# Scratch stores from ScalarE's DMA ring, scratch laid out anew, and weight pairs of four v and five o in a recurrent attention kernel

## The chip, the cores and the metric

The kernel runs on one core of a Trainium2 chip. The metric is the device time of one execution in microseconds (us), lower is better. Each timed execution is one run; profiles come from one profiled execution each. Engines go by their names in the profile: PE is TensorE's matmuls and PEld its weight loads, ACT is ScalarE, DVE VectorE, POOL GpSimd, SP SyncE. A load has *landed* when the last of the 16 increments of its semaphore has come; the trace shows 16 for each load and doesn't name the DMA engines that they come from.

## The reference

Two parts share an input `x` of 2048 rows by 1024. Part A is a recurrence over 64 segments of 32 rows: each segment puts eight memory rows, the first eight output rows of the segment before, in front of its own 32. Part B is a gated feed-forward layer. A gate mixes both.

```python
mem = mem0                                        # 1 x 8 x 1024
for s in range(64):                               # 2048 rows / 32
    h = concat([mem, x[:, 32*s:32*s+32]])         # 40 rows
    q, k, v = h @ Wq, h @ Wk, h @ Wv              # 32 heads of 128: three 1024 x 4096 weights, bf16
    p = softmax(mask(q @ k.T * scale))
    o = (p @ v) @ Wo                              # 4096 x 1024
    mem = o[:, :8]
    outs.append(o[:, 8:])
b = (gelu(x @ w_gate) * (x @ w_up)) @ w_down      # 1024 -> 3584 -> 1024
out = g * a + (1 - g) * b
```

The four weights of part A are 8 MB each and every segment needs all of them; only the memory rows wait for the segment before.

## The kernel before

Each of the four weights is cut into 16 pieces of 0.5 MB: half `r` (16 heads) times row block `i` (0 to 7). The kernel keeps them in 52 slots of SBUF: 40 serve one piece each, and 12 serve a pair of pieces, half 0 and half 1 of the same block. `PAIRS` names which blocks of each weight are paired. The halves change places every other segment, so that a paired slot is loaded once a segment: 12 loads, 6 MB.

```python
PAIRS = {"k": (0, 2), "q": (0,), "v": (0, 1, 2, 3, 4), "o": (0, 1, 2, 3)}

def seq(m, r):            # order of the blocks: paired ones first in the first half, last in the second
    ...
    return p + f if r == 0 else f + p
walk = both(0) + one("v", 0) + both(1) + [x for y in zip(one("o", 0), one("v", 1)) for x in y] + one("o", 1)

def at_step(p, s):
    m, r, i = walk[p]
    return (m, r ^ (s % 2), i)
...
def fetch(n):             # the load of a slot's next piece, on SyncE
    ...
    op("sp", lambda e: e.dma_start(dst(t, k), src(k)), wr=[t.r()], lane=lane)

def spent(k):             # called after the matmuls of a piece
    n = home[k]
    done[n] += 1
    if done[n] < len(uses[n]) and uses[n][done[n]] != k:
        fetch(n)
```

A segment has 64 steps of matmuls (`walk`). The k and q pieces are steps 0 to 15 and 24 to 39, the first v half 16 to 23, the second v half alternates with the first o half in steps 40 to 55, and the second o half is 56 to 63. A slot is loaded again right after the step that used its first piece. So a v pair has some 30 steps until its second piece is needed, while an o pair is freed at step 40 or later and needed from step 59 or 60. The o pairs have the shortest lead of all.

Four intermediate results go through scratch in HBM, all stored by GpSimd:

```python
qk_scr = nc.dram_tensor("qk_scr", [128, NSEG, 4, 128], BF16)
o_scr = nc.dram_tensor("o_scr", [NSEG, 128, 2, 128], BF16)
...
def store_v(u, G, st):
    op("pool", lambda e: e.dma_start(v_scr[4 * G:4 * G + 4, :, u].rearrange("s i (g j) c -> g (s i) (j c)", g=4), st[:, :]), ...)
def o_store(s=s):         # behind step 60
    op("pool", lambda e: e.dma_start(o_scr[s].rearrange("p u c -> p (u c)"), oRc[:, :, :, :].rearrange("p u c x -> p (u c x)")), ...)
for p in range(64):
    run(at.get(p, []))
    proj(p, s)
... # a_bf <- PB[XO] by ACT and DVE; transposed by PE into the next segment's input
def a_store(s=s):
    op("pool", lambda e: e.dma_start(a_scr[s].rearrange("r (g c) -> g r c", g=4), a_bf[:, :]), ...)
```

## Time and profile before

| kernel before | value |
|---|---|
| runs | 2225.03 to 2231.35 us, median 2227.73 of 3 |
| span of the profiled run, granted clock | 2225.5 us, 0.990 |
| recurrence, 64 segments | about 110 to 1640 us |
| period of a segment | 24.48 us |

The prediction below shows the windows of the stages and the chain. Here are more views of the kernel before. The first is from its page: the granted clock of TensorE (PE) in 40 slices, in tenths; the groups of the v and o projections (L800 and L811), with busy time, mean ns of one, idle time just before them and what ended most of it; and the DMA queues (q1 is fed by SyncE, q0 by GpSimd, q10 by ScalarE), with packets, MB and their share of the 16 engines.

```profile
PEclk9999999999999999999999999999999999999999
...
q1 hardware_dynamic: 216240, 483.68, 62.2%
q0 software_dynamic: 22400, 40.56, 5.6%
q10 hardware_dynamic: 144, 0.26, 0.1%
...
L800 PE MATMUL pb<-sl,hT 128*32 128x512 bf16 x8192 | 728.1, 382 | 49.1 <-DMA sl<-in_A_Wv_dram 37.0
L811 PE MATMUL pb<-sl,oT 128*32 128x256 bf16 x8192 | 352.8, 276 | 85.0 <-DMA sl<-in_A_Wo_dram 47.6
```

Most DMA traffic is the weight loads on q1 (820 of 0.5 MB, 430 of 529 MB). PE waits for v and for o loads, and for both not long (37.0 and 47.6 us in all). The waits of PE and of its weight loads (PEld) show the same; the numbers are total us, times, and the longest. A weight load and a matmul can wait for the same transfer, so the two engines' rows are not to be added.

```profile
PEld pb L800 <- DMA sl<-in_A_Wv_dram: 61.4, 85, 2.0
PEld pb L811 <- DMA sl<-in_A_Wo_dram: 56.7, 54, 2.5
PE pb L754 <- DVE vA L679: 17.4, 29, 1.8
```

### The profile page before, as it was taken

The page shows a single profiled execution, that of the slowest core. Times are in us where ns is not written, and L with a number is a line of the kernel's source. Part 1 is how long each engine was busy: PE and PEld are TensorE (multiplying, and loading weights), DVE is VectorE, ACT ScalarE, POOL GpSimd, SP SyncE. Part 2 cuts the span into 40 slices and gives each one's busy share as a digit, 9 for nine tenths or more (in the row PEclk, how much of TensorE's full clock was granted, in tenths as well). Part 3 has the DMA queues.
Part 4 walks back from the last instruction along what each step waited for, and adds up shares of the span by engine and source line. Part 5 has one row for each costly group of instructions (what it writes and reads, how often), then busy time and mean ns, then how long its engine had stood idle before and what let it go on. Part 6 is the DMA issues. An engine that isn't in the chain of part 4 may idle for free.

```text
span 2225.5 us, 77508 instructions
## 1 busy us (share of the span) xinstructions
PE 2008.3 (90%) x38220; PEld 936.1 (42%) x32556; DVE 1016.7 (46%) x2248; ACT 597.7 (27%) x1266; POOL 431.1 (19%) x776
## 2 busy tenths in 40 slices
PE   7878888988898888888988898899888999999999
PEld 4334444444444434444444444444444424343343
DVE  6434444444444444444444454444444516354362
ACT  4322222222222222222222232222222303122130
POOL 7221222221222222122222222222221000000000
PEclk9999999999999999999999999999999999999999
DMA  9988887888788878888888888788889400001000
GB/s 365 356 287 278 298 292 274 287 302 290 263 292 305 286 265 289 288 294 271 301 289 280 272 310 296 267 294 305 279 287 369 164 34 29 30 25 34 20 29 20
DMA packets 239111, 529.46 MB, mean 238 GB/s; under 512 B 46760, under 2 KB 79784, under 8 KB 238784
## 3 DMA queue, kind: packets, MB, share of 16 engines
q1 hardware_dynamic: 216240, 483.68, 62.2%
q0 software_dynamic: 22400, 40.56, 5.6%
q8 instruction: 278, 4.55, 0.8%
q10 hardware_dynamic: 144, 0.26, 0.1%
q14 instruction: 49, 0.40, 0.1%
HBM read 490.68 MB, written 33.55 MB: 236 GB/s over the span
## 4 chain that ended last, share of the span: by engine, by line
PE 57%; DMA 29%; DVE 9%; issue 2%; ACT 2%; SPq 1%; POOL 0%; POOLq 0%; DVEq 0%; ACTq 0%
DMA sl<-in_A_Wo_dram 18%; PE pb L462 16%; PE pb L800 11%; PE pb L783 9%; DMA sl<-in_A_Wk_dram 6%; PE pb L811 5%; PE pb L1153 4%; PE pb L690 4%; PE pb L830 3%; DMA sl<-in_A_Wv_dram 2%; PE pb L849 1%; DVE pb L726 1%; PE pb L1131 1%; DVE st L725 1%; DVE st L731 1%
## 5 line engine op out<-in xcount | busy, mean ns | idle before, releaser
L800 PE MATMUL pb<-sl,hT 128*32 128x512 bf16 x8192 | 728.1, 382 | 49.1 <-DMA sl<-in_A_Wv_dram 37.0
L811 PE MATMUL pb<-sl,oT 128*32 128x256 bf16 x8192 | 352.8, 276 | 85.0 <-DMA sl<-in_A_Wo_dram 47.6
L783 PE MATMUL pb<-sl,hT 128*32 128x512 bf16 x4096 | 401.2, 382 | 0.0
L800 PEld LDWEIGHTS pb<-sl,hT 128*32 128x32 bf16 x8192 | 215.5, 97 | 405.2 <-issue 249.9
L811 PEld LDWEIGHTS pb<-sl,oT 128*32 128x32 bf16 x8192 | 208.6, 97 | 174.2 <-issue 58.2
L830 PE MATMUL pb<-sl,hR 128*32 128x512 bf16 x3072 | 221.4, 387 | 11.8 <-ACT stv L676 6.0
L777 POOL COPY oRc<-oT 128x128 bf16<-128x128 bf16 x128 | 97.7, 763 | 648.3 <-DVE oT L679 648.3
L676 ACT ACTIVATE tok<-pb 128x512 bf16<-128x512 f32 x192 | 114.7, 598 | 269.5 <-PE pb L800 255.8
L462 PE MATMUL pb<-xT,wg 128*128 128x512 bf16 x768 | 183.2, 382 | 4.2 <-DMA wg<-in_B_w_gate_dram 4.2
L462 PE MATMUL pb<-xT,wu 128*128 128x512 bf16 x768 | 182.4, 381 | 0.0
L679 DVE CAST stg<-pb 128x512 bf16<-128x512 f32 x128 | 86.3, 674 | 165.1 <-PE pb L783 165.1
L1153 PE MATMUL pb<-wd,GT 128*32 128x512 bf16 x1568 | 152.2, 379 | 0.0
L783 PE MATMUL pb<-wd,GT 128*32 128x512 bf16 x1568 | 152.2, 379 | 0.0
L450 ACT ACTIVATE s<-pb 128x512 f32<-128x512 f32 x112 | 66.9, 597 | 291.2 <-PE pb L462 291.2
L451 DVE SCALAR_TENSOR_TENSOR tp<-s,pb 128x512 f32<-128x512 f32 x112 | 76.8, 685 | 122.8 <-ACT s L450 122.4
L679 DVE CAST a_bf<-pb 128x128 bf16<-128x128 f32 x64 | 18.7, 292 | 245.2 <-ACT a_bf L676 245.2
L676 ACT ACTIVATE oT<-pb 128x256 bf16<-128x256 f32 x256 | 84.3, 381 | 124.7 <-PE pb L766 124.7
L462 PEld LDWEIGHTS pb<-xT,wg 128*128 128x128 bf16 x768 | 75.1, 98 | 96.9 <-issue 8.2
L679 DVE COPY qT<-pb 128x512 bf16<-128x512 bf16 x128 | 54.4, 425 | 133.3 <-ACT kT L676 133.3
L729 ACT ACTIVATE E<-pb 128x320 bf16<-128x320 f32 x128 | 56.0, 437 | 220.4 <-DVE pb L726 220.4
L830 PEld LDWEIGHTS pb<-sl,hR 128*32 128x32 bf16 x3072 | 79.7, 97 | 83.0 <-issue 19.6
L462 PEld LDWEIGHTS pb<-xT,wu 128*128 128x128 bf16 x768 | 75.5, 98 | 91.6 <-issue 1.8
(110 smaller groups left out, 2265.4 us busy)
## 6 DMA issues: line engine op xcount, KB each, us to landing
sl<-in_A_Wv_dram SPq DMA_DIRECT2D x331, 512.0 KB, 8.8
sl<-in_A_Wo_dram SPq DMA_DIRECT2D x268, 512.0 KB, 7.0
sl<-in_A_Wk_dram SPq DMA_DIRECT2D x142, 512.0 KB, 6.7
sl<-in_A_Wq_dram SPq DMA_DIRECT2D x79, 512.0 KB, 7.1
qkr<-qk_scr SPq DMA_DIRECT2D x63, 128.0 KB, 8.1
qk_scr<-fqk POOLq DMA_DIRECT2D x30, 256.0 KB, 6.8
wd<-in_B_w_down_dram SPq DMA_DIRECT2D x7, 1024.0 KB, 14.9
xq_scr<-xTp SPq DMA_DIRECT2D x4, 1024.0 KB, 16.8
```

Of the source, the lines that this page charges most:

```text
L450: op("act", lambda e: e.activation(s1[:, :], hg, ACTF.Square, scale=SQ), rd=[BK(bg)], wr=[s1.r()])
L451: op("dve", lambda e: e.scalar_tensor_tensor(out=t[:, :], in0=s1[:, :], scalar=1.0, in1=hg, op0=ALU.add, op1=ALU.mult), rd=[BK(bg), s1.r() ...
L462: ins = e.matmul(PB[bk][:, 0:FB], lhsT=w[:, kc, cc:cc + 128], rhs=x[:, :, :, kc, :].rearrange("p t i c -> p (t i) c"), start=(kc == 0), st ...
L676: op("act", lambda e: e.activation(o, i, ACTF.Copy), rd=rd, wr=wr)
L679: op("dve", lambda e: e.tensor_copy(o, i), rd=rd, wr=wr)
L690: ins = e.transpose(to, t[:, j * 128:(j + 1) * 128], ident[:, :])
L777: op("pool", lambda e: e.tensor_copy(oRc[:, u, :, :].rearrange("p c (g j) -> p g j c", g=4), diag), rd=[oT.r()], wr=[oRc.r(128 * u, 128 * ...
L783: return e.add_instruction(mybir.InstMatmult(name=nc.get_next_instruction_name(), start_tensor_calc=start, stop_tensor_calc=stop, tile_siz ...
L800: ins = again(e, g, *at, one, end) if k[0] == "q" else e.matmul(*at, start=one, stop=end)
L811: ins = e.matmul(PB[XO][32 * g:32 * g + 32, 0:256], lhsT=oT[:, gp_, 2 * jj + hh, 0:32], rhs=w[:, c:c + 256], start=(r == 0 and one and hh ...
L830: ins = e.matmul(PB[b][32 * g:32 * g + 32, :], lhsT=h[:, k[2], :], rhs=w[:, g * 512:(g + 1) * 512], start=(n == 0), stop=(n == 7))
L1153: ins = again(e, q, *a, j == 0, j == NJ - 1) if hf else e.matmul(*a, start=(j == 0), stop=(j == NJ - 1))
```

## The change

The intent: take the stores off GpSimd's software ring and issue them from ScalarE (ACT); lay out the q/k scratch so that each partition is stored as one row of 2 KB, and the o scratch so that each is read as one row of 1 KB (a q/k read becomes two rows of 512 B where it was one of 1 KB); and move one pair from v, for which PE waits 61 us, to o. The number of loads stays 12.

```diff
-        qk_scr = nc.dram_tensor("qk_scr", [128, NSEG, 4, 128], BF16)
+        qk_scr = nc.dram_tensor("qk_scr", [NG, 2, 128, 4, 256], BF16)
-        o_scr = nc.dram_tensor("o_scr", [NSEG, 128, 2, 128], BF16)
+        o_scr = nc.dram_tensor("o_scr", [NG, 2, 128, 4, 128], BF16)
 ... (the q/k and o reads follow the new layouts)
-        PAIRS = {"k": (0, 2), "q": (0,), "v": (0, 1, 2, 3, 4), "o": (0, 1, 2, 3)}
+        PAIRS = {"k": (0, 2), "q": (0,), "v": (0, 1, 2, 3), "o": (0, 1, 2, 3, 4)}
 ...
-        def store_v(u, G, st):
-            op("pool", lambda e: e.dma_start(v_scr[...]...
+        def store_v(u, G, st, eng="act"):
+            op(eng, lambda e: e.dma_start(v_scr[...]...
-        def store_qk(u, G, st):
-            op("pool", lambda e: e.dma_start(qk_scr[:, 4 * G:4 * G + 4, 2 * u:2 * u + 2, :]...
+        def store_qk(u, G, st, eng="act"):
+            op(eng, lambda e: e.dma_start(qk_scr[G, u].rearrange("p i c -> p (i c)"), ...
 ... (the stores of the prologue stay on "pool")
             def o_store(s=s):
-                op("pool", lambda e: e.dma_start(o_scr[s].rearrange("p u c -> p (u c)"), ...
+                op("act", lambda e: e.dma_start(o_scr[s // 4, :, :, s % 4, :].rearrange("u p c -> p u c"), ...
             def a_store(s=s):
-                op("pool", lambda e: e.dma_start(a_scr[s].rearrange("r (g c) -> g r c", g=4), a_bf[:, :]), ...
+                op("act", lambda e: e.dma_start(a_scr[s].rearrange("r (g c) -> g r c", g=4), a_bf[:, :]), ...
```

More of the change, by code (lines that the diff above doesn't have):

```diff
@@ L532, in load_qk @@
         def load_qk(s):
-            op("sp", lambda e: e.dma_start(qkr[:, :, :, :].rearrange("p u m c -> p (u m c)"), qk_scr[:, s].rearrange("p m c -> p (m c)")),
+            op("sp", lambda e: e.dma_start(qkr[:, :, :, :].rearrange("p u m c -> p u (m c)"),
+                                           qk_scr[s // 4, :, :, s % 4, :].rearrange("u p c -> p u c")),
                rd=[("D", "qk", s // 4, u) for u in range(2)], wr=[qkr.r()], lane="qkr")
@@ L663, in load_oR @@
         def load_oR(Q, u, t=oR):
-            op("pool", lambda e: e.dma_start(t[:, :, :].rearrange("p (s i) x -> p s (i x)", i=NB),
-                                             o_scr[4 * Q:4 * Q + 4, :, u, :].rearrange("s p c -> p s c")),
+            op("pool", lambda e: e.dma_start(t[:, :, :].rearrange("p a x -> p (a x)"), o_scr[Q, u].rearrange("p s c -> p (s c)")),
                rd=[("D", "o", s) for s in range(4 * Q, 4 * Q + 4)], wr=[t.r()], lane="oR")
@@ L867, in fill_put @@
                     [BK(TT)], [r])
-        def store_v(u, G, st):
-            op("pool", lambda e: e.dma_start(v_scr[4 * G:4 * G + 4, :, u].rearrange("s i (g j) c -> g (s i) (j c)", g=4), st[:, :]), rd=[st.r()],
-               wr=[("D", "v", G, u)], lane="fv")
-        def store_qk(u, G, st):
-            op("pool", lambda e: e.dma_start(qk_scr[:, 4 * G:4 * G + 4, 2 * u:2 * u + 2, :].rearrange("p i m y -> p i (m y)"),
-                                             st[:, :, :, :].rearrange("p i m y -> p i (m y)")),
-               rd=[st.r()], wr=[("D", "qk", G, u)], lane="fq")
+        def store_v(u, G, st, eng="act"):
+            op(eng, lambda e: e.dma_start(v_scr[4 * G:4 * G + 4, :, u].rearrange("s i (g j) c -> g (s i) (j c)", g=4), st[:, :]), rd=[st.r()],
+               wr=[("D", "v", G, u)], lane=f"fv{eng}")
+        def store_qk(u, G, st, eng="act"):
+            op(eng, lambda e: e.dma_start(qk_scr[G, u].rearrange("p i c -> p (i c)"), st[:, :, :, :].rearrange("p i m y -> p (i m y)")),
+               rd=[st.r()], wr=[("D", "qk", G, u)], lane=f"fq{eng}")
         def mm0(m, u, b, t, G=0, h=hR):
@@ L882, in mm0 @@
             if m == "v":
-                store_v(u, G, t)
+                store_v(u, G, t, "pool")
         def tr0(m, u, t, b, G=0):
@@ L892, in tr0 @@
             if m == "q":
-                store_qk(u, G, b)
+                store_qk(u, G, b, "pool")
         def rest_k(u):
@@ L1008, in o_store @@
             def o_store(s=s):
-                op("pool", lambda e: e.dma_start(o_scr[s].rearrange("p u c -> p (u c)"), oRc[:, :, :, :].rearrange("p u c x -> p (u c x)")),
+                op("act", lambda e: e.dma_start(o_scr[s // 4, :, :, s % 4, :].rearrange("u p c -> p u c"),
+                                                oRc[:, :, :, :].rearrange("p u c x -> p u (c x)")),
                    rd=[oRc.r()], wr=[("D", "o", s)], lane="sto")
@@ L1037, in a_store @@
             def a_store(s=s):
-                op("pool", lambda e: e.dma_start(a_scr[s].rearrange("r (g c) -> g r c", g=4), a_bf[:, :]), rd=[a_bf.r()],
+                op("act", lambda e: e.dma_start(a_scr[s].rearrange("r (g c) -> g r c", g=4), a_bf[:, :]), rd=[a_bf.r()],
                    wr=[("D", "a", s)], lane="st")
```

## The prediction

> **What bounds the kernel now.** I began with the table of windows, which cuts the span into its stages. Its columns are the window in us, its length, busy time of PE, weight loads, DVE, ACT and POOL with instruction counts, the granted clock, the busy share of the DMA engines, and GB/s.
>
> ```profile
> 0.00:110.00 110.00, 88.39 (x700) 42.49 (x668) 59.08 (x92) 40.74 (x74) 51.58 (x60) 0.97 0.97 361
> 110.00:1640.00 1530.00, 1352.79 (x31751) 666.68 (x27776) 695.78 (x1749) 427.51 (x974) 348.98 (x661) 0.99 0.84 287
> 1640.00:1720.00 80.00, 66.01 (x1084) 33.09 (x987) 35.14 (x74) 20.24 (x41) 11.86 (x21) 0.94 0.98 340
> 1720.00:2225.50 505.50, 501.08 (x4698) 193.86 (x3127) 226.67 (x333) 109.19 (x178) 18.65 (x34) 1.00 0.13 46
> ```
>
> The second row is the 64-segment recurrence, and all of the change lies there. PE is busy 1352.8/1530 = 88%, so 12%, or 177 us (2.8 us a segment), is the most that any change of transfers can give. In the feed-forward tail PE is at 99%; nothing of the change acts there.
>
> Next, one segment in the same view:
>
> ```profile
> 1051.20:1054.00 2.80, 2.67 (x72) 1.47 (x64) 0.46 (x2) 0.86 (x3) 1.24 (x3) 1.00 0.21 69
> 1057.00:1060.00 3.00, 3.00 (x80) 1.42 (x64) 0.97 (x3) 1.19 (x2) 0.29 (x1) 1.00 0.93 272
> 1063.00:1066.00 3.00, 3.00 (x83) 1.79 (x76) 2.00 (x5) 1.70 (x4) 0.97 (x2) 1.00 1.02 403
> 1045.00:1048.00 3.00, 2.29 (x64) 1.27 (x68) 2.38 (x9) 0.78 (x3) 0.00 (x0) 1.00 1.04 392
> ```
>
> The DMA engines are full (0.93 to 1.04) in all but one stretch, 1051.2 to 1054.0, at the turn from one segment to the next. The chain of waits that ended last has the same shape: one load of output weights (Wo) nearly every segment.
>
> ```profile
> by line: DMA sl<-in_A_Wo_dram 18.5%; PE pb L462 16.1%; PE pb L800 11.5%; PE pb L783 8.6%; DMA sl<-in_A_Wk_dram 5.6%; PE pb L811 5.1%; PE pb L1153 3.8%; PE pb L690 3.6%; PE pb L830 2.7%; DMA sl<-in_A_Wv_dram 2.4%; issue 2.4%; PE pb L849 1.2%
> ...
> 1043.26 7.84 DMA sl<-in_A_Wo_dram
> ```
>
> Those 7.8 us are mostly time spent queued behind other loads. I averaged issues and landings of the 12 weight loads (0.5 MB each) over the 64 segments. Counted from the first k load, the k,q,k loads are issued at 0, 0.39, 1.07 us and land at 4.80, 7.39, 8.90; the five v loads are issued at 3.8 to 6.1 and land at 10.83, 12.24, 13.64, 15.03, 16.41; the four o loads are issued at 12.4 to 14.2 and land at 17.95, 19.43, 20.83, 22.36. Then 2.27 us pass to the next first k load; the period is 24.6 us. So when the first o load is issued, the fifth v load still has 4.0 us to go: the queue never runs dry, and **the bound is the total of bytes through a busy queue plus one bubble per segment**. In the bubble PE finishes the output projection, ACT and DVE copy it out, it is transposed into the next input, the first k step frees its slot, and the first packets come some 1 us later.
>
> [...] of the v store issued at 751.08, twelve of 16 increments came after 1.86 to 2.27 us and four after 4.17 to 4.44. [...] the median SyncE packet took 18 ns at 256 B, 27 at 512 B, 46 at 1 KB, 84 at 2 KB and 159 at 4 KB.
>
> **The change, part by part.**
> *Stores leave GpSimd.* By the order of instructions, 187 issues move from POOL to ACT (64 o, 64 a, 30 v, 29 k/q: 2.9 a segment). A POOL issue took 0.57 to 0.78 us; POOL is 19% busy and not in the chain, so freeing 187 x 0.65 = 122 us of it is worth about 0. On ACT an issue should cost about what SyncE needs, 0.35 to 0.6 us; ACT is busy 28% of this stage. The o store comes ahead of the copy of a, where ACT has waited:
>
> ```profile
> ACT a_bf L676 <- PE pb L811: 217.0, 64, 4.8
> POOL qk_scr L874 <- DVE fqk L679: 89.0, 29, 4.6
> ```
>
> that is 217/64 = 3.4 us each segment; one or two issues (up to 1.2 us) fit. The a store comes after the copy into the next input, with about 2.9 us until ACT's next copy. Cost: 0.
>
> *The same bytes, on other engines.* From GpSimd, o and v stores moved in the bubble, free. From ACT they start about 0.5 us earlier and meet the tail of the o loads. v: 128 KB on four engines is 32 packets of 1 KB each, 32 x 46 ns = 1.5 us, in about half the segments; perhaps 0.2 us of it lies ahead of the last o landing: 0.1 us on average. o: 256 packets of 256 B over 16 engines, 16 x 18 ns = 0.3 us, of which 0.05. a: 32 packets of 512 B on each of four engines, 32 x 27 = 0.86 us, where it was four packets of 4 KB, 4 x 159 = 0.64, [...] 0.1 to 0.2 us. Together about +0.3 us a segment at most, x64 = 19 us; I take half, **+10 us**, as the end of the busy stretch is set by the slowest of 16 engines, which need not be these.
>
> *The layouts.* k/q store: 512 rows of 512 B become 128 of 2 KB; o reads: 512 of 256 B become 128 of 1 KB. But GpSimd's packets were already merged to 4 KB (9,840 of them on its queue), so this saves little. On the way back, the q/k read goes from 128 x 1 KB to 256 x 512 B, 16 x 27 - 8 x 46 = +64 ns a segment, after the o loads, in the bubble: 0. k/q bytes, 256 KB in half of the segments, still meet the k and v loads: 0.
>
> *Pairs.* One v load fewer and one o load more per segment: 12 loads still. The o rows are 2 KB: 2 x 84 = 168 ns per 4 KB against 159. In the landings above, v loads stand 1.39 us apart and o loads 1.49. So +0.1 us x 64 = **+6 us**. Back the other way, the last v load lands 1.4 us earlier; PE waited for v 37 us and its weight loads 61, but in most segments the o wait that follows simply gets longer by as much. In the chain, only about four segments hang on v: 4 x 0.7 = **-3 us**. The fifth o slot is freed two steps (some 0.5 us) after the fourth, and its load is queued behind four others, so the later issue costs 0. Would the queue run dry? The fourth v load lands at 15.0 and the first o load is issued at 12.4 [...]: a margin of 0.6 us, enough on average.
>
> Sum: 10 + 6 - 3 = **+13 us**, 2241. That adds only costs that I can see, and relieving GpSimd's software ring may give back what I can't; I take 10 us off for that. This is a judgement, not a reading. **2231 us.**
>
> **Rivals.** *A, [...]* If the a and v stores all fall on the same four engines, their lag (0.86 + 0.75 on average) counts in full: +1.0 us x 64 = +64 us, 2290. For it: every load waits for its slowest engine. Against it: half of this falls in the bubble. *B, the software ring was slowing the loads.* 2.5 to 5 us after the first k load, just after the a store, the loads run at about 200 GB/s, and at 380 to 400 later. If leaving GpSimd ended that, it would give about 1.1 us x 64 = -70 us, 2160. Against it: while the k/q store moves, 6 to 8 us after the first k load, its packets take 159 ns and loads beside it run at full pace, so stores from GpSimd alone do not make the dip; and it is there in all four phases. *C, ACT becomes late.* If an issue takes over 1.5 us, the copy of a is late by the rest: +0.5 us, +32 us. Against it: the 3.4 us of idle time. *D, o is the wrong matrix to pair.* Its lead, from slot freed to use, is the shortest. If the queue runs dry before o, one more load of 1.4 us is exposed in part of the segments, say a third: +30 us, 2258.
>
> **Range and chances.** 2% is 44.6 us, or 0.7 us in each segment. My parts are a third of that; only A or B in full reaches it. I give 2231 us, 2200 to 2262, with 0.06 faster, 0.87 same and 0.07 slower.
>
> **What would show it.** Right: the period stays at 24.3 to 25 us; the Wo wait still leads the chain, and v waits shrink while PE's o waits grow; the turn of segments keeps its hole of about 3 us; POOL's issues are gone and ACT's busy time is unchanged. a and v stores from ACT post twelve increments at once. Wrong: the first k load lands over 0.7 us later (A) or the 200 GB/s dip is gone (B); ACT's copy of a starts late after an issue (C); the DMA share drops between the v and the o loads (D).

## More of the kernel before

The timeline of SyncE's queue in one segment, whose first k load was issued at 1029.20 us, has this row for its o loads (start, duration of the four issues):

```profile
1041.65 1.98 SPq L378 DMA_DIRECT2D sl<-in_A_Wo_dram  x4
```

So the o loads are asked for 12.45 us after the first k load: at that time their slots come free.

## The result and the profile after

The changed kernel takes **2335.75 us** (median of four runs, 2331.7 to 2346.05), where the kernel before takes 2226.38 in the same rounds (2218.8 to 2231.35). The ratio is 1.050, with a 95% interval of 1.045 to 1.055: slower by 5%. A ratio is the mean time of one kernel's runs over that of the other's of the same rounds, so it is not quite the ratio of the medians quoted. Executions over 1.5% slower than the fastest of the same kernel are left out of the means. The profiled run has a span of 2344.3 us, where before had 2225.5: +118.8.

The windows of the stages, kernel after, with the columns explained in the prediction:

```profile
110.00:1740.00 1630.00, 1390.26 (x31480) 668.55 (x27544) 687.19 (x1736) 427.50 (x965) 214.26 (x475) 0.95 0.80 267
1830.00:2344.00 514.00, 507.79 (x4838) 198.62 (x3270) 229.20 (x338) 110.87 (x181) 18.67 (x34) 1.00 0.15 53
```

Cut there, the window of the recurrence is 1630 us long instead of 1530. The cuts are by eye, but the loads confirm them: from the first k load of the last segment to the end it is 565.7 us before and 566.1 after, so all of the +118.8 lies in the recurrence. Three columns of the first row moved: the granted clock from 0.99 to 0.95, the DMA share from 0.84 to 0.80, and PE's busy time from 1353 to 1390 us for slightly fewer instructions. The page of the kernel after, with the lines that answer to those of before:

```profile
PEclk9989999999999999999999999999988999999999
...
q1 hardware_dynamic: 232640, 484.20, 60.5%
q10 hardware_dynamic: 34136, 20.19, 3.0%
q0 software_dynamic: 8592, 20.49, 2.4%
...
DMA sl<-in_A_Wo_dram 22%; PE pb L462 15%; PE pb L800 14%; PE pb L783 10%; PE pb L811 5%; PE pb L690 4%; PE pb L1153 4%; PE pb L830 2%; DMA sl<-in_A_Wk_dram 2%; DVE pb L726 1%; DVE st L725 1%; PE pb L849 1%; DVE st L731 1%; DMA qkr<-qk_scr 1%; DVE tB L742 1%
...
L800 PE MATMUL pb<-sl,hT 128*32 128x512 bf16 x8192 | 751.5, 394 | 4.8 <-DMA sl<-in_A_Wk_dram 2.6
L811 PE MATMUL pb<-sl,oT 128*32 128x256 bf16 x8192 | 365.4, 277 | 153.8 <-DMA sl<-in_A_Wo_dram 142.0
```

The stores did move: 20 MB went from q0 to q10. The same 8192 matmuls of L800 take 394 ns on average where they took 382, though one digit a slice hides most of the lower clock. The idle time before v matmuls went from 49 to 5 us, that before o matmuls from 85 to 154, and the o load has 22% of the chain instead of 18%. The waits of the kernel after:

```profile
PEld pb L811 <- DMA sl<-in_A_Wo_dram: 161.1, 127, 2.8
PE pb L811 <- DMA sl<-in_A_Wo_dram: 142.0, 150, 2.6
PE pb L754 <- DVE vA L679: 62.6, 63, 2.0
PEld pb L800 <- DMA sl<-in_A_Wv_dram: 1.4, 5, 0.4
ACT a_bf L676 <- PE pb L811: 286.4, 60, 7.0
```

The wait for v is gone, as the change meant. The wait of L754 (attention) for DVE's copy of v grew at the same time, from 17.4 us to 62.6; that the one became the other isn't shown. The wait for o tripled. ACT still waits for PE before its copy of `a`, 286.4 us in all, so its new issues don't hold it up.

One segment of the kernel after, whose first k load was issued at 1045.03 us, in the timeline of SyncE's queue and then in windows:

```profile
1056.81 2.99 SPq L378 DMA_DIRECT2D sl<-in_A_Wo_dram  x5
```

```profile
1054.00:1056.80 2.80, 2.60 (x60) 1.36 (x56) 2.35 (x7) 1.58 (x4) 0.32 (x1) 1.00 0.99 399
1056.80:1059.00 2.20, 2.20 (x84) 1.70 (x80) 1.18 (x3) 0.27 (x1) 0.68 (x2) 1.00 0.61 181
1059.00:1062.00 3.00, 2.40 (x60) 1.25 (x48) 2.36 (x8) 0.82 (x2) 0.00 (x0) 1.00 1.02 387
1065.00:1068.00 3.00, 1.34 (x34) 0.55 (x32) 0.00 (x0) 0.11 (x1) 0.15 (x1) 1.00 0.60 163
```

From 1056.8, when the first o load is issued, to 1059.0 the engines are busy for only 0.61 of the time and move 181 GB/s, with 399 just ahead and 387 just after. The lost bytes come back at the end: at 1065 to 1068 PE is busy for 1.34 of 3.00 us, waiting for the last o loads. In the kernel before, where the first o load was issued at 1041.65, the same view has

```profile
1042.00:1045.00 3.00, 2.95 (x100) 1.99 (x88) 1.78 (x4) 0.44 (x1) 0.28 (x2) 1.00 0.94 342
```

and 1.04 for 1045 to 1048 (shown in the prediction).

To see it over all segments, I averaged over segments 4 and later the times at which loads land, in us after the first k load is issued. This table is worked out from the traces (e1, e9 and e13 are experiments below). Its last column counts the stretches in which PE was granted half its clock: in before each of the 5 lasts 3.41 us; in after 34 last 3.41, three 6.83 and one 10.24.

| kernel | first o issued | last v landed | o loads landed | period | half-clock windows |
|---|---|---|---|---|---|
| before (5 v, 4 o) | 12.25 | 16.32 | 17.79, 19.26, 20.66, 22.19 | 24.48 | 5 |
| after (4 v, 5 o) | 12.68 | 14.92 | 17.10, 18.98, 20.74, 22.29, 23.82 | 26.33 | 38 |
| e1, pairs alone | 12.77 | 15.14 | 17.23, 19.12, 20.91, 22.40, 23.86 | 26.4 | 38 |
| e9, e1 with PE kept busy | 12.18 | 14.77 | 16.70, 18.43, 20.05, 21.62, 23.09 | 25.55 | 2 |
| e13 (3 v, 6 o) | 12.83 | 13.96 | 16.96, 18.63, 20.66, 22.21, 23.63, 25.18 | 27.95 | 56 |

The fourth v load lands at 14.93 us before and 14.92 after: up to there nothing is lost. The remaining five loads then take 7.26 us before (22.19 - 14.93) and 8.90 after. That is 1.64 us a segment, or 105 us in 64; the other 0.2 us of the period is the turn from the last o landing to the next k issue (2.29 us before, 2.50 after). The rate of the loads in the same time base:

```
GB/s of the weight loads, by the start of a 0.5 us bin after the first k issue (worked out from the traces)
          11.0  11.5  12.0  12.5  13.0  13.5  14.0  14.5  15.0
before     389   372   399   406   368   321   297   333   349
after      398   367   290   193   132   121   168   251   326
e1         400   382   329   248   173   149   181   249   308
e9         392   356   313   218   165   195   259   328   349
e13        267   185   119    78    60    77   135   230   311
```

Before has a dent of a quarter at 13.5 to 14.5; after has a hole of two thirds. In the segment shown above, the 16 increments of the fourth v load and of the first o load came at these times:

```
us after its own issue (worked out from the trace of the kernel after)
v, issued 1050.07   6.98 7.11 7.15 7.31 7.32 7.33 7.36 7.46 7.63 7.70 7.92 7.95 8.29 8.49 9.03 9.28
o, issued 1056.81   3.29 3.31 3.32 3.33 3.34 3.37 3.48 3.49 3.51 3.54 3.59 3.74 3.77 3.88 4.02 4.90
```

The first increment of v came at 1057.05, half of them by 1057.5, the last at 1059.35. The o load had been issued before any of this, and still its first increment did not come before 1060.10. On average over the segments the first increment of v comes at 12.56 us and half of them have come at 13.18; the first o packet starts at 13.76, 1.06 us after its issue.

### The profile page after: what moved, and what is told of

It reads as the page before. It is cut to its first block, busy times and chain, and to the rows that moved or that the text cites. A ratio compares the mean times of both kernels' runs of the same rounds, so it can differ in the third digit from the quotient of the medians.

```text
span 2344.3 us, 77525 instructions
## 1 busy us (share of the span) xinstructions
PE 2057.8 (88%) x38218; PEld 944.3 (40%) x32556; DVE 1014.3 (43%) x2248; ACT 601.1 (26%) x1266; POOL 294.1 (13%) x589
## 4 chain that ended last, share of the span: by engine, by line
PE 58%; DMA 28%; DVE 10%; ACT 2%; issue 1%; POOL 0%; SPq 0%; ACTq 0%; POOLq 0%; DVEq 0%
DMA sl<-in_A_Wo_dram 22%; PE pb L462 15%; PE pb L800 14%; PE pb L783 10%; PE pb L811 5%; PE pb L690 4%; PE pb L1153 4%; PE pb L830 2%; DMA sl<-in_A_Wk_dram 2%; DVE pb L726 1%; DVE st L725 1%; PE pb L849 1%; DVE st L731 1%; DMA qkr<-qk_scr 1%; DVE tB L742 1%
## 5 line engine op out<-in xcount | busy, mean ns | idle before, releaser
L800 PE MATMUL pb<-sl,hT 128*32 128x512 bf16 x8192 | 751.5, 394 | 4.8 <-DMA sl<-in_A_Wk_dram 2.6
L811 PE MATMUL pb<-sl,oT 128*32 128x256 bf16 x8192 | 365.4, 277 | 153.8 <-DMA sl<-in_A_Wo_dram 142.0
L783 PE MATMUL pb<-sl,hT 128*32 128x512 bf16 x4096 | 422.6, 403 | 0.0
L800 PEld LDWEIGHTS pb<-sl,hT 128*32 128x32 bf16 x8192 | 219.7, 100 | 372.4 <-issue 296.1
L811 PEld LDWEIGHTS pb<-sl,oT 128*32 128x32 bf16 x8192 | 199.2, 97 | 260.6 <-DMA sl<-in_A_Wo_dram 161.1
L830 PE MATMUL pb<-sl,hR 128*32 128x512 bf16 x3072 | 228.0, 400 | 11.1 <-ACT stv L676 7.0
L895 POOL COPY kT<-qkr 128x128 bf16<-128x128 bf16 x128 | 37.7, 295 | 676.1 <-PE pb L719 484.1
```

What stands on the lines that cost most here:

```text
L783: return e.add_instruction(mybir.InstMatmult(name=nc.get_next_instruction_name(), start_tensor_calc=start, stop_tensor_calc=stop, tile_siz ...
L800: ins = again(e, g, *at, one, end) if k[0] == "q" else e.matmul(*at, start=one, stop=end)
L811: ins = e.matmul(PB[XO][32 * g:32 * g + 32, 0:256], lhsT=oT[:, gp_, 2 * jj + hh, 0:32], rhs=w[:, c:c + 256], start=(r == 0 and one and hh ...
L830: ins = e.matmul(PB[b][32 * g:32 * g + 32, :], lhsT=h[:, k[2], :], rhs=w[:, g * 512:(g + 1) * 512], start=(n == 0), stop=(n == 7))
```

## The experiments

Fifteen kernels were run, all correct. The first question is which part of the change costs the time; then why.

### Which part: e1, e2, e14, e15

**e1: the pairs alone**, on the kernel before.

```diff
-        PAIRS = {"k": (0, 2), "q": (0,), "v": (0, 1, 2, 3, 4), "o": (0, 1, 2, 3)}
+        PAIRS = {"k": (0, 2), "q": (0,), "v": (0, 1, 2, 3), "o": (0, 1, 2, 3, 4)}
```

> The kernel before with nothing but the weight pairs changed to 4 v and 5 o; all stores stay on GpSimd, scratch layouts as before. Theory 1 (the load queue runs dry between the fourth v load and the first o load, and starts up slowly again; the longer wait at the end of the segment then also costs the PE clock): it carries nearly all of the loss, 2310 to 2340 us, with the DMA rate falling under 200 GB/s some 12.5 to 14 us after the first k load, and a granted clock of 0.95 to 0.97. Theory 2 ([...] ScalarE late because it issues): this kernel is about 2232 us, as the prediction's sum has +6 for the pairs.

Measured: 2330.62 us, ratio 1.049 (1.045 to 1.053), half-clock windows and landings like those of after (table above).

**e2: stores and layouts**, the whole change with `PAIRS` put back.

```diff
-        PAIRS = {"k": (0, 2), "q": (0,), "v": (0, 1, 2, 3), "o": (0, 1, 2, 3, 4)}
+        PAIRS = {"k": (0, 2), "q": (0,), "v": (0, 1, 2, 3, 4), "o": (0, 1, 2, 3)}
```

> The changed kernel with the weight pairs put back to 5 v and 4 o: stores on ScalarE's ring and the new scratch layouts. Theory 1: within 1% of the kernel before, 2215 to 2245 us, clock 0.98 to 0.99. Theory 2: 2300 us or more, with the o loads landing later and the first k load late.

Measured: 2229.86 us, ratio 1.003 (1.001 to 1.006). The window of its recurrence has the length, the DMA share and the clock of before:

```profile
110.00:1640.00 1530.00, 1354.18 (x31716) 670.75 (x27756) 695.72 (x1747) 430.85 (x972) 215.23 (x478) 0.99 0.84 287
```

So the pairs carry +109 us (0.0488 x 2225) and the rest +7. The one line of the change that alters neither the number of loads, nor their bytes, nor any engine's work is the one that counts.

**e14 and e15** split the rest, with five rounds each: the new layouts with all stores left on GpSimd, and the old layouts with the stores on ACT.

```diff
 # e14 on the kernel before: qk_scr, o_scr and their reads as in the change, and
+        def store_v(u, G, st, eng="pool"):
+        def store_qk(u, G, st, eng="pool"):
 # e15 on the kernel before: PAIRS, qk_scr, o_scr and reads untouched, and
+        def store_v(u, G, st, eng="act"):
+        def store_qk(u, G, st, eng="act"):
-                op("pool", ...o_scr...)   -                op("pool", ...a_scr...)
+                op("act", ...o_scr...)    +                op("act", ...a_scr...)
```

> The new scratch layouts alone, stores on GpSimd and pairs 5 v and 4 o as before. By the prediction's sum 0; fewer rows for the software ring might give a little: 2215 to 2232 us (0.995 to 1.003 of the kernel before).

> The stores on ScalarE's ring alone, old layouts and pairs. The two parts together took 1.003 (e2). [...] this one is 1.003 to 1.006 and the layouts alone at or below 1.000; if the layouts make it, this one is 1.000.

Measured: 2228.59 us, 0.998 (0.996 to 1.001), and 2225.43 us, 0.998 (0.995 to 1.000). Neither can be told from the kernel before, and the two don't add up to the +7 us of e2. So of the stores and layouts together no more can be said than that they are worth less than 0.6% either way. No version beats the kernel before.

### Is it the number of o pairs: e3, e4, e13

One rival to a queue that runs dry is that an o load is simply dearer than a v load (its rows in HBM are shorter: in before the median packet of q1 took 84 ns at 2 KB, so 168 for 4 KB, and 159 at 4 KB). Then each o pair more should cost, and each one fewer should gain.

```diff
-        PAIRS = {"k": (0, 2), "q": (0,), "v": (0, 1, 2, 3, 4), "o": (0, 1, 2, 3)}
+        PAIRS = {"k": (0, 2), "q": (0,), "v": (0, 1, 2, 3, 4, 5), "o": (0, 1, 2)}      # e3
+        PAIRS = {"k": (0, 2, 4), "q": (0,), "v": (0, 1, 2, 3), "o": (0, 1, 2, 3)}      # e4
+        PAIRS = {"k": (0, 2), "q": (0,), "v": (0, 1, 2), "o": (0, 1, 2, 3, 4, 5)}      # e13
```

> The kernel before with the pairs moved the other way, 6 v and 3 o. Theory 1: nine loads stand ahead of the first o load, so the queue can't run dry; the sum of bytes is the same, so 2205 to 2235 us; the rate between v and o stays over 300 GB/s. If instead an o pair is dear by itself (2 KB rows, the shortest time from slot freed to use), each one fewer gives back what one more cost: some 100 us faster, about 2120 us.

Measured: 2231.81 us, 1.002 (0.999 to 1.005). No gain, so an o load as such is not dear. The rate stays above 370 GB/s from the v loads to the o loads, so here the queue doesn't run dry at all. The waits of PE's weight loads show why there is none: the wait only changed the matrix, from 57 us for o and 61 for v before to

```profile
PEld pb L800 <- DMA sl<-in_A_Wv_dram: 169.2, 189, 2.3
...
PEld pb L811 <- DMA sl<-in_A_Wo_dram: 3.6, 6, 1.2
```

> The kernel before with one v pair given to k: 3 k, 4 v, 4 o. v has four pairs as in the changed kernel, but eight loads stand ahead of the first o load as in the kernel before. Theory 1 (what counts is how much is queued ahead of the o loads): 2210 to 2245 us. If the loss comes from having only four v pairs (order of v work on TensorE): 2310 to 2340 us.

Measured: 2257.61 us, 1.015 (1.013 to 1.017). This missed its range from 2210 to 2245 by some 12 us. With four v and four o pairs the o loads are issued later (13.19 us, for PE waits for the fourth k load), and the last v load lands at 15.92, only 2.7 us after the first o issue; before it was 4.1 us. Here again the o loads stand far apart when that lead is short (17.79, 19.44, 21.15, 22.60).

> A further dose on the kernel before: 3 v and 6 o, so that six loads stand ahead of the first o load (8 in the kernel before, 7 in e1). If it is the queue that runs dry: it is dry some 1.4 us a segment longer than in e1 (2331 us), so 2385 to 2440 us, with the first o load landing over 2.5 us after the last v load. If e1's loss were a fixed charge (another order of the output projection, a clock that has dropped once), about 2331 to 2350.

Measured: 2444.55 us, 1.096 (1.093 to 1.099), just above the range. With 4, 5 and 6 o pairs the cost is 0, 109 and 214 us (0.0958 x 2230). At 6 the rate falls to 60 GB/s, and the clock to 0.92 in the recurrence:

```profile
110.00:1820.00 1710.00, 1423.28 (x31140) 668.89 (x27268) 680.93 (x1719) 419.83 (x956) 343.92 (x649) 0.92 0.75 252
```

The share of 0.84, 0.80 (after) and 0.75 falls in step. Together with e3 this fits a queue that runs empty ahead of the o loads, the more so the fewer v loads are ahead of them.

### The clock: e5, e6, e9, e10

The other thing that moved is PE's clock. From segment 4 on the trace of before has it at half in 5 stretches (17 us in all), that of after in 38 (147 us). No long gap of PE goes with them: with matmuls and weight loads taken together, its longest gap from segment 4 on was 2.8 us in before, 2.6 in after and 2.9 in e1, which has 38 such stretches too. In the 3.4 us ahead of a half-clock stretch of after PE's busy share was 0.37 on average (0.56 at most), where it is 0.85 over the recurrence: a low share went with them. What sets the clock isn't shown. To learn what part these stretches have in the loss, idle matmuls with the identity were put ahead of steps 60 to 63, where PE waits for o. They write a bank that is free then.

```diff
             for p in range(64):
                 run(at.get(p, []))
+                if p in (60, 61, 62, 63) and not last:
+                    def spin(e):
+                        for _ in range(9):                      # e5 on e1, e6 on before: nine of 128 x 128
+                            ins = e.matmul(PB[B0][:, 0:128], lhsT=ident[:, :], rhs=ident[:, :], start=True, stop=True)
+                        return ins
+                    op("pe", spin, rd=[ident.r()], wr=[BK(B0)])
                 proj(p, s)
 # e9 on e1, e10 on before: two of 128 x 512 instead (the identity repeated four times)
```

> e1 (pairs alone) with nine idle 128x128 matmuls (some 0.5 us) put ahead of each of the last four o steps of a segment, where TensorE waits for the o loads anyway; they write a bank that nothing reads. In e1 the clock was at half in 38 windows of a segment's turn (5 in the kernel before), and the first o load was issued 0.5 us later. If the half clock carries a part of the loss: fewer than 15 such windows, the o issue back at 12.3 us, and some 0.6 us a segment less, about 2290 us. If it is only a sign of the wait: 2325 to 2350 us whatever the clock does.

Measured: 2333.91 us, 1.048 (1.043 to 1.053), the same as e1. Half-clock windows fell from 38 to 3 or 4 and the o loads were issued at 12.17 us again, but a block of nine small matmuls, each with its own weight load, took 0.68 us (I had expected 0.5), and part of it lay in the turn to the next segment (2.74 us from the last o landing to the next k issue; e1: 2.49).

> The control for e5: the kernel before with the same idle matmuls. Its waits for o are 1.3 us a segment, so up to 0.7 us of the 2 us of matmuls may show: 2225 to 2265 us under either theory.

Measured: 2314.29 us, 1.039 (1.033 to 1.045): a miss, I expected at most 2265. In the kernel before PE hardly waits there (47.6 us for o in all, where after has 142.0), so that the same work lies in the turn, which grew from 2.29 to 4.03 us. The pair e5/e6 doesn't measure the clock: the idle work is too dear. All it shows is that in e1 the idle work and what it brings cancel.

> e5 with cheaper idle work, as e6 showed that 36 small matmuls with 36 weight loads took a microsecond ahead of the last o step: now two 128x512 matmuls (some 0.5 us) ahead of each of the last four o steps, on the pairs-alone kernel. If the half clock carries a part of the loss of e1 (2331 us): under 15 half-rate windows, first o load issued at 12.2 to 12.4 us and 20 to 40 us gained, 2290 to 2310. If the clock is only a sign of the wait: 2325 to 2345.

Measured: 2303.0 us, 1.031 (1.026 to 1.036), as expected. The clock is back at 0.99 and PE's busy time includes the idle work:

```profile
110.00:1710.00 1600.00, 1479.79 (x32244) 683.16 (x28276) 693.24 (x1749) 427.08 (x973) 349.44 (x661) 0.99 0.81 275
```

Against e1 that is -28 us by medians, -39 by ratios (0.0177 x 2225). If the idle work by itself only costs time, as I take it, the lost clock is worth at least 28 to 39 us of e1's 109: an estimate from these two differences. The table of landings shows how: with full clock the o loads are issued 0.6 us earlier (12.18, not 12.77), and the o loads land earlier by 0.5 to 0.9 us. But the first o load still lands 1.9 us after the last v load, where before it is 1.5, and five landings are still wide apart. The clock is not all.

> Control for e9: the kernel before with the same idle matmuls, which find only 1.3 us of wait for o: 2220 to 2255 us. What it loses bounds what the matmuls cost by themselves.

Measured: 2306.23 us, 1.033 (1.028 to 1.039): a miss again, for the reason of e6 (turn 3.78 us). A use it has: with the same idle work in both, 5 v/4 o and 4 v/5 o take the same time. That is not evidence that the clock is the whole, since the idle work lies in a wait in one and in the turn in the other.

### The dry queue: e7, e8, e11, e12

If the queue is empty for some time in each segment of e1, a load more should cost little there, and its full time in the kernel before. So a resident piece of q is loaded once more in each segment, ahead of the v loads, with the data that it already holds: 13 loads.

```diff
             spent(k)
+            if k[0] == "q" and walk[p][1] == 0 and end and 1 <= s < NSEG - 1:
+                fetch(home[k])                                  # e7 on before, e8 on e1, e11 on e9
```

> The kernel before with one useless load more in each of 62 segments: a q weight slot that stays resident is loaded again with its own data (0.5 MB), issued just before the v loads. The queue is full in the kernel before, so every load costs its time: 62 x 1.4 us = +87 us, about 2312 us.

Measured: 2291.05 us, 1.029 (1.024 to 1.034), +64 us (0.0289 x 2225) for 62 loads: 1.0 us for each, less than the 1.1 us by which I came to 2312, and less than the 1.4 us between landings.

> e1 (pairs alone) with the same useless load, issued just before the v loads, so that eight loads again stand ahead of the first o load. If the queue runs dry there and the start-up after it is what costs, the added 0.5 MB is free or better: 2295 to 2330 us, the rate between v and o stays over 280 GB/s. If e1's loss is bytes or o's slower packets, it adds 1.4 us a segment: about 2415 us.

Measured: 2349.33 us, 1.054 (1.048 to 1.060), 19 us over e1 by medians and 12 by ratios; the profiled runs take 2345.2 and 2343.9, nearly the same. By the rival, that bytes are what count, it would be 2415. The windows of the recurrence in e1, e7 and e8, in this order:

```profile
110.00:1740.00 1630.00, 1396.58 (x31476) 675.07 (x27536) 687.63 (x1736) 425.93 (x966) 347.69 (x657) 0.95 0.79 267
```

```profile
110.00:1690.00 1580.00, 1373.79 (x31504) 651.59 (x27568) 697.53 (x1744) 424.99 (x967) 346.72 (x656) 0.98 0.85 297
```

```profile
110.00:1740.00 1630.00, 1401.62 (x31412) 665.38 (x27472) 689.31 (x1734) 424.32 (x966) 346.09 (x656) 0.95 0.84 287
```

In e8 the same 1630 us hold a load more per segment, at a share of 0.84 instead of 0.79 and at 287 GB/s instead of 267. Its last o load lands at 23.85 us, that of e1 at 23.86: thirteen loads are through when twelve are. The rate between v and o still dips to 272 GB/s, where I had expected over 280. So e1 has a hole that takes a load of 64 us for 12 to 19. **About 45 to 50 us of e1's loss is this hole**, with some 15 us of uncertainty from the intervals. (The range I had set ended at 2330, so e8 lies slightly above it.)

> Pairs alone with both cures: the useless load ahead of the v loads (the queue stays full, as in e8) and the idle matmuls (the clock stays up). If a queue that runs dry and a clock that drops are the whole loss, this comes down to the kernel before with the same useless load (e7, 2291 us): 2280 to 2315. If something of the pairs is left (the fifth o load's place at the end), 2330 us or more.

Measured: 2324.07 us, 1.041 (1.036 to 1.047); a miss, above 2315. It is what the single effects add up to, 2331 + 19 - 28 = 2322, but it stands 33 us over e7, which has the same 13 loads with 5 v and 4 o pairs. So with the hole nearly filled (a dip to 312 GB/s; e7 stays above 375) and the clock kept up, some 30 us remain. The landings place them: the last five loads take 7.33 us where those of e7 take 6.93, and the turn is 2.45 us where it is 2.17; against that, the last v load lands 0.16 us ahead of e7's eighth load. How much of this is the idle matmuls' own time, no run tells.

One measure orders all of these kernels: the lead, by which the first o load is issued before the last v load lands, and the lowest rate of the weight loads from 11 us on (averages over segments 4 and later, 0.5 us bins, worked out from the traces).

| kernels | lead, us | lowest rate, GB/s |
|---|---|---|
| e3, e7 | 5.5 to 5.6 | 372 to 379 |
| before, e2, e6, e8, e10, e11, e14, e15 | 3.9 to 4.1 | 272 to 324 |
| e4 | 2.7 | 210 |
| after, e1, e5, e9 | 2.2 to 2.6 | 121 to 171 |
| e13 | 1.1 | 68 |

The useless load of e8 lifts the lead of e1 from 2.4 to 3.9 us, and the hole shrinks to a dip. No run changed the time of the o issue alone.

**e12** asks why the loads start slowly. After an o issue into an empty queue the rate needs some 2 us to come back (after: o issued at 12.68, 121 GB/s at 13.5, 326 at 15.0), and q1 is slow as well 2.5 to 5 us after the first k load (226 GB/s in before, 217 in after). If that is because the queue was idle in the turn, two loads of no use issued into the turn should end it.

```diff
+                if 1 <= s < NSEG - 2:                           # on the kernel before, behind the last load of a segment
+                    for j in (6, 7):
+                        on("o", 1, 0, lambda k=("v", s % 2, j): fetch(home[k]))
```

> A test of the slow start-up, on the kernel before: two useless loads (resident v slots with their own data, 1 MB) issued after the last load of a segment, so that the DMA engines stay busy across the turn of segments. If loads are slow after an idle queue (200 GB/s, packets of 270 ns, from 2.5 to 5 us after the first k load), the second and third k/q load then land 1 us earlier: 2160 to 2220 us in spite of 64 MB more. If the slow stretch belongs to the k and q loads themselves, the added loads only get in their way: 2240 to 2310 us.

Measured: 2267.86 us, 1.016 (1.010 to 1.023). The slow stretch stays, with packets of 4 KB at 256 ns on average (3 to 5 us after the k issue) where the v stretch has 161; the median is 159 in both, so it is a part of the packets that takes far longer. The second and third loads (q and k) land at 8.01 and 9.35 us, even later than before (7.32 and 8.84). But the test was not clean: the useless loads were themselves issued only 2.3 us before the last o load landed, the rate fell to 113 GB/s ahead of them, and they ran at 190 to 258 GB/s through the turn. It shows that loads under way through the turn didn't end the slow start; whether an idle queue begins it, and what else could, stays open.

## Why the prediction was wrong

The time was predicted at 2231 us, 2200 to 2262, with 0.07 for slower by over 2%. It is 2336.

- **What bounds the kernel: right in the main for before, not for after.** A busy queue plus a bubble: e7 agrees, a load more costs 1.0 us of each segment. But "full (0.93 to 1.04) in all but one stretch" was read from some of the windows: 1054 to 1057 has 0.81 and 1048 to 1051.2 has 0.84, and the averaged rate dips to 297 GB/s at 14.0. The queue was already near its limit. The error was to carry "busy" over to the changed kernel, where it is so no longer.
- **Stores leave GpSimd, cost 0: right.** Those issues are gone, and no path noticed (e15: 0.998).
- **Same bytes on other engines, +10 us: not seen.** With the layouts it is +2 to +13 us (e2), but alone it is -10 to +1 us (e15), so the term was small, as foreseen, and its sign isn't known. The a and v stores from ACT show one update of their semaphore early (0.9 us after issue for a) and four later (2.3 to 2.4 us for a). In before the same stores show 16 updates; if they add up to as much here, the first stands for twelve, as foreseen. An ACT issue took 0.34 to 0.52 us by the medians of the four kinds, about the 0.35 to 0.6 foreseen.
- **Layouts, 0: right** (e14: 0.998).
- **Pairs, +6 - 3 = +3 us: this term measured +109 (e1).** Within it, "+0.1 us x 64" for the dearer o rows is not what failed (e3: one o pair fewer is worth nothing). What failed is the step "**Would the queue run dry? The fourth v load lands at 15.0 and the first o load is issued at 12.4**", with "a margin of 0.6 us, enough on average". That margin allows for the time to the first data an estimate of mine that no trace shows. The last v load does land at 14.92 and the first o load is issued at 12.68, nearly as put. But the time to the first data is not the measure, nor is it what was wrong: the first o packet starts 1.06 us after its issue, within the 2.24 us from that issue to the last v landing (14.92 - 12.68). A load has landed with the last of its 16 increments; the first of the fourth v load come 2 us and more before the last (1057.05 to 1059.35 in the segment shown; 12.56 to 14.95 us on average, so the first comes before the o load is even issued), and the rate falls from 12 us on, to 121 GB/s at 13.5. And a load into a queue that runs empty needs far longer than these 1.06 us to land. The prediction itself had the number: the first k load, issued into an empty queue, lands at 4.80 us. In after the first o load lands 17.10 - 12.68 = 4.42 us after its issue, in e1 4.46, in e9 4.52, in e13 4.13. At one spacing of 1.4 us behind the fourth v load it would have landed at 16.3 to 16.4. The 0.7 to 0.8 us between, times 64, is 45 to 51 us, what e8 against e7 gives for the hole.
- **Rival D had the mechanism and the wrong size.** "one more load of 1.4 us is exposed in part of the segments, say a third: +30 us". Between 12 and 16 us after the first k issue the rate falls below 200 GB/s for a microsecond in 59 of the 61 segments from segment 4 on (before: 6 of 61), and the sign that it named, a lower DMA share between the v and the o loads, is there: 0.61.
- **A term was missing: the clock.** A wait for o at the end of the segment, in place of two shorter ones for v and for o, goes with a lower clock: half-clock stretches went from 5 to 38, and e9, with idle matmuls in that wait, has 2. I had not looked at whether longer waits would bring one. It goes with a later issue of the very loads that PE waits for (12.77 us in e1, against 12.18 in e9). At least 28 to 39 us.
- **Waits.** "The last v load lands 1.4 us earlier" was right, and so was "the o wait that follows simply gets longer by as much", but it got longer by more: PE's own wait for o went from 48 to 142 us, for 37 us less on v.
- **Rivals A, B, C: not seen.** A: the first k load landed at 4.97 instead of 4.70 us, not 0.7 later. B: the slow start after the k loads is still there. C: ACT is still early for its copy of a, as its wait of 286.4 us shows.

The account of e1's +109 us: hole in the queue about 45 to 50, clock at least 28 to 39, and about 20 to 30 that I can't assign. The added load and the idle matmuls change the time by the sum of their single effects in e11, so hole and clock were not counted twice to any large extent. Shown by experiment: the pairs alone do it; the queue has room in e1 that it hasn't in the kernel before; the clock is part of it. Shown by the order of the leads, but not by a run that moves the o issue alone: that the hole comes from the o loads being issued too late behind the v loads. Argued from landings only: that the 4.4 us from issue to landing is the right measure for it. Open: the rest, and why loads start slowly.

## What to carry to other kernels

Ask of a queue of loads how long before the last load ahead lands the next one is issued, and compare this lead with the **time that a load into an empty queue takes to land**, not with the time to its first data (1.06 us here). In these kernels that time was 4.1 to 5.0 us; a lead of 5.5 us left no dip, one of 3.9 to 4.1 a shallow one (before: 4.07, 16.32 - 12.25), and one of 2.7 or less a hole (after: 2.24). No run lies between 4.1 and 5.5 us, so where exactly the dip begins isn't shown. So moving a load from a matrix with a long lead to one with a short lead is not neutral, even if it ends a visible wait: first compare the lead of both with that number. And ask of each lengthened wait of PE whether it can lower its clock (here from 0.99 to 0.95 in the recurrence), as the very issues that end the wait then come later (12.77 us in e1, 12.18 in e9).
